# A retention and swish kernel on one core: batches 0 and 1 load their keys and values two positions a partition

## The chip, the core and the metric

The kernel runs on one core of a Trainium2 chip. TensorE (PE) multiplies matrices, VectorE (DVE), ScalarE (ACT) and GpSimd (POOL) work element by element, and SyncE (SP) issues nearly all DMAs. The metric is the device time of one execution, in microseconds. It is given as the median of several runs; the profile comes from one further execution.

## The reference

The kernel computes a retention layer over 8 batches, 8 heads, 576 positions and a head size of 64, and then a dense block with a swish in it:

```python
scores = scale * np.matmul(q, k.transpose(0, 1, 3, 2))
gamma = 1.0 - 2.0 ** (-5.0 - np.arange(H, dtype=np.float32))
rel = pos[:, None] - pos[None, :]
Dmat = np.where(rel >= 0, gamma[:, None, None] ** rel[None, :, :], 0.0)
attn_out = np.matmul(scores * Dmat[None, :, :, :], v)
x = attn_out.transpose(0, 2, 1, 3).reshape(B * S, H * D)      # 4608 x 512
h = x @ w_in                                                  # 512 x 2048
g = h * (1.0 / (1.0 + np.exp(-beta * h)))
return (g @ w_out).astype(np.float32)                         # 2048 x 512
```

All inputs and the output are float32 in DRAM. The kernel works in bf16 on TensorE.

## The kernel before

The decay factorizes: gamma to the power (i - j) is a gain on query i (`gq`) times a gain on value j (`gv`), so each batch needs only a causal mask. The first 512 positions of a batch are four chunks of 128; the last 64 of all batches together form a ninth block. A chunk's output has two parts: scores of the chunk against itself, masked and multiplied with its values (`a_sc`, `a_O`), and the queries times a state, the sum of key-value products of all chunks before it (`a_st`, `a_cross`). The output of the four chunks of a batch stands transposed in `xT`, and is the input of the dense block: 16 "ups" (`up`, `ups`) of four matmuls of 512 columns each, whose result goes through a Silu on ScalarE into `gT`, and then "downs" (`down`). From block 3 on the downs are done by a scheme with seven products in place of eight (`seven_mm`).

Queries lie four positions a partition: position 4 s + i is in partition s, slot i, so that a chunk of 128 positions is a group of 32 partitions (`PC`) in each of four slots. A DMA of q moves pieces of 1 KB (`load_q`, L77 to L87, two DMAs of 512 KB, by halves of the heads). Keys and values of batches 0 and 1 (`b < QB`) lie one position a partition, so `load_kv` (L89 to L105) moves pieces of 256 bytes; a chunk's keys and values share one tile `kvn` of 512 KB, of which there are six. Batches 2 to 7 use another layout with half chunks side by side, and are not touched.

Batches 0 and 1 work by chunk. For each chunk `pre` (L330) casts the keys to bf16 (`kn`, L364) and multiplies the values with `gv` (`vn`, L336), both on GpSimd; `t_k` (L391) transposes the keys on TensorE and copies them out of PSUM into `kT`; `a_sc` (L403) makes the scores of a chunk in 8 matmuls with 64 rows and 128 columns of the array and masks them on VectorE into `R` (L417); `a_O` (L449) makes 8 matmuls with 128 rows and 64 columns; `a_st` (L474) adds to the state in 4 matmuls of the whole array and copies its two diagonal blocks into `sbd`; `a_cross` (L437) multiplies the state with the queries; `a_x` (L464) copies the output into `xT`. `t_q` (L384) transposes the scaled queries that `pre_q` (L310) writes. `warm_up` (L259) issues float32 matmuls on zeros as fillers.

Every engine runs its instructions in the order in which the program issues them. The order for batch 0 is written out by hand (L869 to L915). The rest is a list `fill` of TensorE steps in order, with side steps merged in: each side step has a due place in that list (`streams`, L957 to L972; `merged`, L857), `d0` being the place of the first down and `u1` that of batch 1's first up. SP's queue has the same order. PSUM has eight banks, held by tag: "mm" three, "O" two, "sc" two, "st" one; a step waits until the bank that it takes over has been copied out.

The weights come behind batch 0: eleven DMAs of `w_in` (`load_w_in`, L192) in eight pieces, 4 MB in all, cast to bf16 by GpSimd and VectorE in turn (`cast_w_in`, L201), then `w_out`. The first ups need the cast of the first piece. Batch 1's loads follow `w_out` at place 10.3 of the list, and batch 2's follow them.

Of the kernel before, what the change touches and what calls it, by code (L numbers as in the profile page):

```python
# [19 lines left out]
def kernel(  # L20
# [54 lines left out]
    q_tiles, kv_tiles = {}, {}  # L75
# [13 lines left out]
    def load_kv(n, js=(0, 1)):  # L89

        if n >= len(full):
            return
        b, c = seq[full[n]]
        if 0 in js:
            kv_tiles[full[n]] = stage.tile([P, 2, H, D], F32, name="kvn", tag="kvn", bufs=NQ)
        t = kv_tiles[full[n]]
        for j in js:
            src = (k, v)[j][b].rearrange("h s d -> s h d")
            if b < QB:
                nc.sync.dma_start(t[:, j], src[c * P:(c + 1) * P])  # L100
            elif c % 2 == 0:
# [6 lines left out]
    ahead = [(0, 0), (0, 1), (1, 0), (1, 1), (2, 0), (3, 0), (2, 1), (3, 1)]  # L108
    keys_first = [(0, 0), (1, 0), (0, 1), (1, 1), (2, 0), (3, 0), (2, 1), (3, 1)]
# [12 lines left out]
    load_q(0)  # L122
    for n, j in ahead:
        load_kv(n, (j,))
# [9 lines left out]
    for j, (step, mul) in enumerate(((1, CB), (P, 1))):  # L134
        nc.gpsimd.iota(pos[:, j, :CB], pattern=[[step, CB]], base=0, channel_multiplier=mul,
# [10 lines left out]
    for h in range(H):  # L146
# [12 lines left out]
    causal = consts.tile([P, P], BF16, name="causal")  # L159
    nc.gpsimd.memset(causal[:], 1.0)  # L160
    nc.gpsimd.affine_select(out=causal[:], in_=causal[:], pattern=[[1, CB], [CB, PC]], compare_op=ALU.is_ge,
                            fill=0.0, base=0, channel_multiplier=-1)
# [38 lines left out]
    def cast_w_in(g, kos=None):  # L201
        t = wts[g]
        f0, fn, rows = pieces[g]
        for ko in kos or range(rows[0].start, rows[-1].stop):
            if ko % 2 == 0:
# [59 lines left out]
    def betas():  # L265
        pb = psum.tile([P, FO], F32, name="pb", tag="mm", bufs=3)
        nc.tensor.transpose(pb[:], beta_rows[:], ident_f[:FO, :FO])
        nc.scalar.copy(beta_sb[:], pb[:])
# [24 lines left out]
    def row_of(b, c):  # L293
        return CB + 1 + c % 2 * 2 + c // 2 if b >= QB else c
# [35 lines left out]
    def pre(i, js=(0, 1)):  # L330

        b, c = seq[i]
        if 0 not in js:
            v, g = kv_tiles.pop(i)[:, 1], gains(gv, row_of(b, c))
            if b < QB:
                nc.gpsimd.tensor_tensor(live[i]["vn"][:], v, g, ALU.mult)  # L336
            else:
                by_halves(live[i]["vn"], v, g)
# [24 lines left out]
        for to, hs in turned if b >= QB else [(slice(0, H), slice(0, H))]:  # L363
            nc.gpsimd.tensor_copy(kn[:, c % 2, to], t[:, 0, hs])  # L364
        if 1 in js:
            pre(i, (1,))

# [16 lines left out]
    def t_q(b, u):  # L384
        T = psum.tile([P, CB, 2, P], BF16, name="T", tag="mm" if u else "O", bufs=3 if u else 2)
        for i in range(CB):
            for p in range(2):
                nc.tensor.transpose(T[:, i, p, :], heads(batch[b]["qs"][:, i], 2 * u + p), ident[:])
        (nc.vector.tensor_copy if u else nc.scalar.copy)(batch[b]["qT"][:, :, 2 * u:2 * u + 2], T[:])

    def t_k(i):  # L391
        T = psum.tile([P, HP, P], BF16, name="T", tag="sc" if i in (CB + 2, CB + 3) else "O", bufs=2)
        for p in range(HP):
            nc.tensor.transpose(T[:, p, :], heads(live[i]["kn"], p), ident[:])
        (nc.vector.tensor_copy if i in (CB + 2, CB + 3) else nc.scalar.copy)(live[i]["kT"], T[:])
# [7 lines left out]
    def a_sc(i):  # L403
        L = live[i]
        L["R"] = R = sb.tile([P, 2, HP, P], BF16, name="R", tag="R", bufs=3)

        tag = "mm" if i == CB - 1 else "O" if i >= E and (i - E) % 2 else "sc"
        sc = [psum.tile([P, HP, P], F32, name="sc", tag=tag, bufs=3 if tag == "mm" else 2) for _ in range(2)]
        for p in range(HP):
            for j in range(2):  # L410
                r = slice(j * D, (j + 1) * D)
                rhs, view = q_cols(i, r, p)
                nc.tensor.matmul(view(sc[j][:, p, :]), L["kT"][r, p, :], rhs, start=True, stop=True,  # L413
                                 skip_group_check=True)
        m_b = causal[:].unsqueeze(1).to_broadcast([P, HP, P])
        for j in range(2):
            nc.vector.tensor_tensor(R[:, j], sc[j][:], m_b, ALU.mult)  # L417

    def split(i):
        return i in (CB - 1, CB + 1)  # L420

    def new_O(i):
        b, c = seq[i]
        if split(i):
            tags = ("sc", "sc") if i == CB - 1 else ("O", "sc")
            live[i]["O"] = [psum.tile([P, 2, P], F32, name="O", tag=t, bufs=2) for t in tags]
# [22 lines left out]
    def a_O(i):  # L449

        b, c = seq[i]
        L = live[i]

        early = i < E
        if not early:
            new_O(i)
        R, vn = L["R"], L["vn"]
        crossed = c > 0
        for j, p in [(n % 2, n // 2) for n in range(H)]:
            nc.tensor.matmul(O_of(i, p)[j * D:(j + 1) * D], vn[:, 2 * p + j, :], R[:, j, p, :],  # L460
                             start=opens(i, p) and not (early and crossed), stop=early or not crossed,
                             skip_group_check=True)

    def a_x(i):  # L464
# [3 lines left out]
        if split(i):  # L468
            nc.vector.tensor_copy(x[:, :2], view(Os[0]))
            nc.scalar.copy(x[:, 2:], view(Os[1]))  # L470
# [3 lines left out]
    def a_st(i):  # L474

        b, c = seq[i]
        L = live[i]
        if c == 0:
            state_ps[b] = psum.tile([P, HP, P], F32, name="st", tag="st", bufs=1)
        st = state_ps[b]  # L480
        for p in range(HP):
            nc.tensor.matmul(st[:, p, :], heads(L["kn"], p), heads(L["vn"], p),
                             start=(c == 0 and p == 0), stop=True, skip_group_check=True)
        for j in range(2):
            r, cols = slice(j * D, (j + 1) * D), slice(j * D, (j + 1) * D)
            e = nc.vector.tensor_copy if i in (CB + 2, CB + 3) else nc.scalar.copy
            if c < CB - 1:
                e(sbds[c][r, :, cols], st[r, :, cols])
                continue
            e(ends[b][r, :2], st[r, :2, cols])  # L490
            e(ends[b][(1 - j) * D:(2 - j) * D, 2:], st[r, 2:, cols])
# [331 lines left out]

    pos_, ots, held = {}, {}, []
# [44 lines left out]
    warm_up(5)  # L869
    betas()  # L870
    betas_safe()
    for n in range(4):
        pre_q(0, n)
    t_q(0, 0)
    warm_up(1, 128)
    t_q(0, 1)
    pre(0)
    t_k(0)
    warm_up(2, 128)
    a_sc(0)  # L880
    a_st(0)
    pre(1)
    t_k(1)
    warm_up(1, 128)
    a_cross(0, True)
    a_O(0)
    a_x(0)
    a_sc(1)
    a_cross(1, True)
    pre(2, (0,))  # L890
    t_k(2)
    a_st(1)
    a_O(1)
    pre(3, (0,))
    a_sc(2)
    t_k(3)
    a_x(1)
    warm_up(1, 128)
    a_sc(3)
    a_cross(2, True)  # L900
    pre(2, (1,))
    a_st(2)
    a_O(2)
    a_x(2)
    pre(3, (1,))
    warm_up(2, 128)
    a_cross(3, True)
    a_O(3)
    cast_w_in(0, (0, 1))
    a_x(3)  # L910
    cast_w_in(0, (2, 3))
    a_st(3)
# [10 lines left out]
    fill = [F(ups, 0, (fo, fo + 1), u, tags) for fo, tags in ((0, ("mm", "mm")), (2, ("O", "O")), (4, ("sc", "sc"))) for u in range(2)]  # L923
# [27 lines left out]
    def second(i):  # L951
        for f in (a_O, lambda j: a_cross(j, False), a_x):
            f(i)
            f(i + 1)
        a_st(i + 1)
# [5 lines left out]
               [(10.3, F(load_q, 1))] + [(10.3, F(load_kv, CB + n, (j,))) for n, j in keys_first],  # L961
# [145 lines left out]
```

## Time and profile before

| | us |
|---|---|
| median of 3 runs (291.51 to 293.75) | 291.57 |
| the profiled execution | 292.41 |
| its span on the core | 290.7 |

| stretch of the span | what TensorE does there |
|---|---|
| 0 to 18.44 | fillers and batch 0's retention |
| 18.44 to 32.34 | ups of batch 0 |
| 32.34 to 42.70 | downs of batch 0 |
| 42.70 to 55.95 | batch 1's retention between downs of batch 0 and ups of batch 1 |
| 55.95 to 287.3 | ups, downs and the retention of the other batches |

A line of the order of work has start, duration, engine, line of the kernel, instruction, output tile, input tiles, shape and count; neighbouring instructions of one kind are merged, and brackets give the engine's idle time before and what ended it. The end of a matmul is modelled, some 0.17 us behind the last column, so two groups overlap in the list; differences of starts tell more. A line of the waits has the waiting instruction, what it waited for, the sum in us, how many times and the longest.

### The profile page before, as it was taken

To read this page: it belongs to the slowest core of one execution; us is meant where nothing else is said; L and a number is where in the kernel's file an instruction comes from. 1 tells how busy PE (TensorE), PEld (TensorE's weight loads), DVE (VectorE), ACT (ScalarE), POOL (GpSimd) and SP (SyncE) were. 2 spreads that over 40 slices of the span, in tenths; PEclk is the share of its full clock that TensorE was granted. 3 is DMA by queue.
4 is the path that set the end of the run, shared out by engine and by line. 5 is a ranking of instruction groups with operands and counts; after the bars stand their busy time and mean duration, and the time that the engine had idled before them with its cause. 6 is when DMAs were issued, how large, how long until landed. Compare 5 with 4: busy or idle time off the path is not lost.

```text
span 290.7 us, 8297 instructions
## 1 busy us (share of the span) xinstructions
PE 281.9 (97%) x3433; PEld 175.7 (60%) x3433; DVE 186.1 (64%) x340; ACT 171.5 (59%) x301; POOL 139.1 (48%) x259
## 2 busy tenths in 40 slices
PE   8799999999999998999999999999999999999995
PEld 6554446864544554448854885578547845784584
DVE  6563555804896396279889875995597555642673
ACT  5677546686878872765158625772576156837730
POOL 4766207872499397089759539625088100000000
PEclk9999999999999999999999999999999999999999
DMA  8999999996989999988999989990779430003004
GB/s 213 218 342 386 387 283 233 240 190 123 247 180 246 253 187 201 267 225 214 183 249 265 195 231 260 189 156 2 215 176 142 92 144 3 2 28 119 0 4 143
DMA packets 128886, 54.03 MB, mean 186 GB/s; under 512 B 110400, under 2 KB 121680, under 8 KB 128848
## 3 DMA queue, kind: packets, MB, share of 16 engines
q1 hardware_dynamic: 128816, 53.49, 77.9%
q8 instruction: 27, 0.44, 0.7%
q14 instruction: 11, 0.09, 0.1%
q10 hardware_dynamic: 32, 0.01, 0.0%
HBM read 36.71 MB, written 9.44 MB: 159 GB/s over the span
## 4 chain that ended last, share of the span: by engine, by line
PE 55%; DVE 5%; POOL 4%; DMA 2%; issue 1%; ACT 0%; SPq 0%; DVEq 0%
PE ph L727 27%; PE U L764 10%; PE Z L764 7%; PE W L764 6%; DMA qn<-in_q_dram 2%; DVE sa L748 2%; PE O L509 2%; PE po L837 2%; POOL vn L305 2%; POOL kn L364 1%; PE sc L509 1%; POOL qs L323 1%; PE st L509 1%; DVE gT L732 1%; DVE R L286 1%
## 5 line engine op out<-in xcount | busy, mean ns | idle before, releaser
L727 PE MATMUL ph<-xT,w_in_sb 128*128 128x512 bf16 (+1 forms) x560 | 116.8, 364 | 0.0
L727 PEld LDWEIGHTS <-w_in_sb 128*128 128x128 bf16 x560 | 53.3, 98 | 55.2 <-POOL w_in_sb L206 0.7
L734 ACT ACTIVATE gT<-ph,beta_sb 128x512 bf16<-128x512 f32 (+1 forms) x92 | 58.4, 642 | 42.6 <-PE ph L727 41.8
L764 PEld LDWEIGHTS <-sa 128*128 128x128 bf16 x480 | 46.9, 98 | 5.8 <-issue 0.2
L732 DVE TENSOR_SCALAR gT<-hs,ratio 128x512 bf16<-128x512 f32 x48 | 25.8, 538 | 32.9 <-ACT hs L731 32.6
L364 POOL CAST kn<-kvn 128x128 bf16<-128x128 f32 (+2 forms) x80 | 35.8, 483 | 22.3 <-DMA kvn<-in_k_dram 21.8
L323 POOL TENSOR_TENSOR qs<-qn,gq 128x256 bf16<-128x256 f32 x48 | 30.5, 667 | 33.2 <-DMA qn<-in_q_dram 23.4
L748 DVE TENSOR_TENSOR sa<-gT 128x1024 bf16<-128x1024 bf16 (+1 forms) x54 | 43.9, 854 | 1.4 <-PE Z L764 1.2
L731 ACT ACTIVATE hs<-ph,beta_sb 128x512 f32<-128x512 f32 x48 | 33.0, 688 | 19.0 <-PE ph L727 18.7
L837 PE MATMUL po<-w_out_sb,gT 128*128 128x512 bf16 x192 | 43.5, 379 | 0.0
L305 POOL TENSOR_TENSOR vn<-kvn,gv 128x256 bf16<-128x256 f32 x48 | 34.3, 739 | 1.2 <-DMA kvn<-in_v_dram 0.7
L837 PEld LDWEIGHTS <-gT 128*128 128x128 bf16 x192 | 18.1, 98 | 20.6
L764 PE MATMUL U<-b,sa 128*128 128x256 bf16 x192 | 22.9, 272 | 0.1
L764 PE MATMUL Z<-b,sa 128*128 128x256 bf16 x192 | 22.9, 273 | 0.0
L286 DVE TENSOR_TENSOR R<-sc,late 128x512 bf16<-128x512 f32 x24 | 15.4, 681 | 11.4 <-issue 10.2
L764 PEld LDWEIGHTS <-gT 128*128 128x128 bf16 x192 | 18.7, 98 | 3.5
L248 DVE TENSOR_TENSOR b<-wt 128x512 bf16<-128x512 f32 x20 | 16.4, 880 | 1.9 <-ACT wt L231 1.8
L417 DVE TENSOR_TENSOR R<-sc,causal 128x512 bf16<-128x512 f32 x16 | 10.2, 686 | 4.6 <-PE sc L413 4.5
L819 PE MATMUL ph<-xT,w_in_sb 128*128 128x512 bf16 x56 | 12.4, 379 | 0.2 <-ACT xT L470 0.2
L642 ACT CAST xT<-O 128x512 bf16<-128x512 f32 x19 | 9.8, 599 | 3.5 <-PE O L509 3.5
L764 PE MATMUL W<-b,gT 128*128 128x256 bf16 x96 | 11.5, 273 | 0.0
L764 PE MATMUL U<-b,gT 128*128 128x256 bf16 x96 | 11.5, 273 | 0.0
(118 smaller groups left out, 304.8 us busy)
## 6 DMA issues: line engine op xcount, KB each, us to landing
qn<-in_q_dram SPq DMA_DIRECT2D x16, 512.0 KB, 5.8
out_dram<-ot SPq DMA_DIRECT2D x32, 256.0 KB, 3.3
kvn<-in_k_dram SPq DMA_DIRECT2D x20, 256.0 KB, 5.4
kvn<-in_v_dram SPq DMA_DIRECT2D x20, 256.0 KB, 5.1
wt<-in_moe_w_out_dram SPq DMA_DIRECT2D x8, 512.0 KB, 9.3
kvn<-in_k_dram SPq DMA_DIRECT2D x24, 128.0 KB, 4.0
kvn<-in_v_dram SPq DMA_DIRECT2D x24, 128.0 KB, 3.4
wt<-in_moe_w_in_dram SPq DMA_DIRECT2D x5, 512.0 KB, 8.2
```

Of the source, the lines that this page charges most:

```text
L248: nc.vector.tensor_tensor(to, x, y, op)
L286: return lambda: f(*a)
L305: nc.gpsimd.tensor_tensor(vn[:, hs], v[:, hs], g[:, hs], ALU.mult)
L323: nc.gpsimd.tensor_tensor(batch[b]["qs"][:, cs, to], q_tiles[b][:, hs, cs].rearrange("p h i d -> p i h d"), gq[:, cs, hs].unsqueeze(3).to_ ...
L364: nc.gpsimd.tensor_copy(kn[:, c % 2, to], t[:, 0, hs])
L727: nc.tensor.matmul(ph, w_in_sb[:, ko, fo * P:(fo + 1) * P], xts[m][:, ko, :, w], start=(ko == 0), stop=(ko == KO - 1))
L731: nc.scalar.activation(h, ph, ACT.Silu, scale=beta_sb[:, fo:fo + 1])
L732: nc.vector.tensor_scalar(gts[m][:, fo], h, ratio[:, fo // 2:fo // 2 + 1], None, ALU.mult)
L734: nc.scalar.activation(gts[m][:, fo, :, w], ph, ACT.Silu, scale=beta_sb[:, fo:fo + 1])
L748: nc.vector.tensor_tensor(sums_a[0][:, held_in[j], ks], quarter(m, *x, ks), quarter(m, *y, ks), op)
L764: nc.tensor.matmul(chains[c, n][:, 0 if alone else p], a, sevens[k // 2][:, j - 1, k % 2, :], start=j in (3, 4, 1) and k == 0 and (alone o ...
L837: nc.tensor.matmul(po[:, :nn], gT[:, fo, ms, :], w_out_sb[:, fo, n0:n0 + nn], start=(fo == 0), stop=(fo == FO - 1))
```

## The change

Batches 0 and 1 load keys and values by spans of 256 positions, two positions a partition (`load_span`): position 2 p + r of a span is in partition p, slot r. A DMA moves 512 KB in pieces of 512 bytes, and a tile holds either keys or values. Batch 0's order of loads is: first q half, first keys, second q half, last keys, first values, last values. The rows of `pos` and the mask `causal` follow the layout; the mask now has two slots of 128.

In this layout a half of the partitions of a span is a chunk. So `a_sc`, `a_O` and the states work on 64 x 64 parts of the array, and `a_sc(b, u, y)` makes the scores of both chunks of span u for half of the head pairs, y. The state after chunk 0 and that after chunk 1 are made in one step (`states(b, 0)`) in two parts of one bank. `state_out` does the copies.

Some work changes its engine. In batch 0 one cast of keys is on VectorE and one on ScalarE (before: GpSimd), one product of values is on VectorE, some of the copies of transposes change between ScalarE and VectorE, `beta_sb` is copied by VectorE, chunk 2's output is copied by VectorE alone, and the first piece of `w_in` is cast three parts by GpSimd and one by VectorE. The first filler is one call, then `betas`, then three more.

The first two ups are done by halves of the tokens (`up_spans`): chunks 0 and 1 first, 256 columns a matmul, then chunk 3's state, then chunks 2 and 3. Batch 1's steps come in five groups in place of more, smaller ones: key transposes of span 0 at d0 + 12.6; both scores of span 0 with the first two states at d0 + 14; key transposes of span 1 and the outputs of span 0 at d0 + 15.85 and 15.9; scores of span 1 with the third state at u1 + 1; outputs of span 1 and the last state at u1 + 8.

The diff, cut to its core:

```diff
+    def load_span(b, u, j):
+        t = stage.tile([P, H, 2, D], F32, name="kvn", tag="kvn", bufs=NQ)
+        nc.sync.dma_start(t[:].rearrange("p h r d -> p h (r d)"),
+                          (k, v)[j][b][:, 2 * u * P:2 * (u + 1) * P].rearrange("h (p r) d -> p h (r d)", r=2))
+        span_tiles[b, u, j] = t
...
-    load_q(0)
-    for n, j in ahead:
-        load_kv(n, (j,))
+    load_q(0, (0,))
+    load_span(0, 0, 0)
+    load_q(0, (1,))
+    load_span(0, 1, 0)
+    load_span(0, 0, 1)
+    load_span(0, 1, 1)
...
+    def pre_k(b, u, r, copy=nc.gpsimd.tensor_copy):
...
+        copy(spans[b, u]["kn"][:, r], span_tiles[b, u, 0][:, :, r])
+
+    def pre_v(b, u, r, multiply=nc.gpsimd.tensor_tensor):
+        vn = spans[b, u]["vn"][r] = sb.tile([P, H, D], BF16, name="vn", tag="vn", bufs=7)
+        multiply(vn[:], span_tiles[b, u, 1][:, :, r], gains(gv, 2 * u + r), ALU.mult)
...
+    def t_q(b, u, cs=slice(0, CB), copy=None):
...
+        (copy or (nc.vector.tensor_copy if u == b else nc.scalar.copy))(batch[b]["qT"][:, cs, 2 * u:2 * u + 2], T[:])
+
+    def t_k(b, u, r):
+        late_span = b and u
...
+        (nc.vector.tensor_copy if late_span or b == 0 and u != r else nc.scalar.copy)(spans[b, u]["kT"][:, r], T[:])
...
+    def a_sc(b, u, y, step=None):
...
+        tag = ("O" if b else "mm") if y else "sc"
+        sc = [psum.tile([P, 2, 2, P], F32, name="sc", tag=tag, bufs=3 if tag == "mm" else 2) for _ in range(2)]
+        def one(j, r, pp, x):
+            rhs, view = q_cols(b * CB + 2 * u + x, row_d(j), 2 * y + pp)
+            mm(view(sc[j][half(x), r, pp, :]), L["kT"][row_d(j), r, 2 * y + pp, half(x)], rhs, start=True)
+        paired(*[[F(one, j, r, pp, x ^ j) for r in range(2) for pp in range(2) for x in range(2)] for j in range(2)])
...
+    def a_O(b, u, y, crossed=(), last=True):
+        L = spans[b, u]
+        def one(x, pp, r, hh):
+            i, p = b * CB + 2 * u + x, 2 * y + pp
+            mm(O_of(i, p)[row_d(hh)], L["vn"][r][half(x), 2 * p + hh, :], L["R"][y][half(x), hh, r, pp, :],
+               start=opens(i, p) and r == 0 and x not in crossed, stop=last and r == 1)
+        paired(*[[F(one, x, pp, r, hh ^ x) for pp in range(2) for r in range(2) for hh in range(2)] for x in range(2)])
...
+    def states(b, c):
...
+        for n, rows in ((0, half(0)), (1, slice(0, P))) if c == 0 else ((1, half(c % 2)),):
+            for r in range(2):
+                for p in range(HP):
+                    for j in range(2):
+                        mm(st[row_d(j), n, p, :], L["kn"][rows, r, 2 * p + j, :], L["vn"][r][rows, 2 * p + j, :],
+                           start=c == 0 and n == 0 and p == 0 and r == 0, stop=r == 1)
...
+    def up_spans(fs, u):
...
+        w = slice(u * 2 * PC, (u + 1) * 2 * PC)
+        for kos in (range(2), range(2, KO)):
+            for f in fs:
+                for ko in kos:
+                    nc.tensor.matmul(phs[f][:, :, w], w_in_sb[:, ko, f * P:(f + 1) * P], xts[0][:, ko, :, w],
+                                     start=u == 0 and ko == 0, stop=ko == KO - 1, skip_group_check=True)
...
+    warm_up(1)
     betas()
     betas_safe()
+    warm_up(3)
+    for n in range(2):
         pre_q(0, n)
     t_q(0, 0)
+    pre_k(0, 0, 1, nc.vector.tensor_copy)
+    pre_k(0, 0, 0)
+    t_k(0, 0, 1)
+    t_k(0, 0, 0)
+    for n in range(2, 4):
+        pre_q(0, n)
     warm_up(2, 128)
+    a_sc(0, 0, 0, 0)
+    t_q(0, 1, slice(0, 2), nc.scalar.copy)
+    t_q(0, 1, slice(2, CB), nc.vector.tensor_copy)
+    a_sc(0, 0, 0, 1)
+    pre_k(0, 1, 0)
+    pre_k(0, 1, 1, nc.scalar.copy)
+    warm_up(2, 128)
+    t_k(0, 1, 0)
+    t_k(0, 1, 1)
+    pre_v(0, 0, 0)
+    pre_v(0, 0, 1, nc.vector.tensor_tensor)
+    a_sc(0, 0, 1)
+    warm_up(2, 128)
+    a_sc(0, 1, 0)
+    states(0, 0)
+    state_out(0, 0)
+    state_out(0, 1)
+    for r in range(2):
+        pre_v(0, 1, r)
+    for c in range(2):
+        new_O(c)
+    a_O(0, 0, 0)
+    a_O(0, 0, 1, last=False)
     a_x(0)
+    a_sc(0, 1, 1)
+    a_cross(1, False)
     a_x(1)
+    warm_up(2, 128)
     a_cross(2, True)
+    new_O(3)
+    states(0, 2)
+    state_out(0, 2)
+    cast_w_in(0, (0, 1, 2), True)
+    cast_w_in(0, (3,))
+    a_O(0, 1, 0, (0,))
+    a_O(0, 1, 1, (0,))
+    a_cross(3, False)
     a_x(2)
     a_x(3)
+    up_spans((0, 1), 0)
+    states(0, 3)
+    state_out(0, 3)
     cast_w_in(1)
...
     def second(i):
+        for f in (new_O, lambda j: a_O(1, j % CB // 2, j % 2, last=False), lambda j: a_cross(j, False), a_x):
             f(i)
             f(i + 1)
...
+               [(d0 + 8, F(pre_k, 1, 0, r)) for r in range(2)] + [(d0 + 9, F(pre_v, 1, 0, r)) for r in range(2)] +
+               [(d0 + 12.6, F(t_k, 1, 0, 0)), (d0 + 12.6, F(t_k, 1, 0, 1)), (d0 + 14, F(a_sc, 1, 0, 0)), (d0 + 14, F(a_sc, 1, 0, 1)),
+                (d0 + 14, F(states, 1, 0)), (d0 + 14, F(state_out, 1, 0)), (d0 + 15.9, F(second, 4))],
+               [(d0 + 10, F(pre_k, 1, 1, r)) for r in range(2)] + [(d0 + 12, F(pre_v, 1, 1, r)) for r in range(2)] +
+               [(d0 + 15.85, F(t_k, 1, 1, 0)), (d0 + 15.85, F(t_k, 1, 1, 1)), (u1 + 1, F(a_sc, 1, 1, 0)), (u1 + 1, F(a_sc, 1, 1, 1)),
+                (u1 + 1, F(states, 1, 2)), (u1 + 1, F(state_out, 1, 2)), (u1 + 8, F(second, 6))]]
```

More of the change, by code (lines that the diff above doesn't have):

```diff
@@ L424, in new_O @@
         if split(i):
[L425 to L426 removed]
+            live[i]["O"] = [psum.tile([P, 2, P], F32, name="O", tag=t, bufs=2) for t in (("O", "sc") if b else ("sc", "O"))]
         else:
```

177 lines of the change are left out of this document (63 added, 114 removed).

## The prediction

> **What bounds the kernel now.** I read the page's busy times first, then TensorE's waits, then the order of work in the first 20 us engine by engine, and last the two later places where TensorE stands still or where batch 1 is worked off.
>
> ```profile
> PE 281.9 (97%) x3433; PEld 175.7 (60%) x3433; DVE 186.1 (64%) x340; ACT 171.5 (59%) x301; POOL 139.1 (48%) x259
> ```
>
> TensorE is busy 97%, so what counts is when its useful work starts, how much matmul time there is, and its few stalls. Its order of work at the start (start, duration, line, tile, count, [idle before]):
>
> ```profile
> 1.25 4.64 PE L262 MATMUL ph<-warm 128*128 128x256 f32 x10 [1.25 <-DVE warm L130]
> ...
> 8.84 0.66 PE L262 MATMUL ph<-warm 128*128 128x128 f32 x4
> ...
> 17.52 0.41 PE L460 MATMUL O<-R,vn 128*64 128x128 bf16 x8
> 17.87 0.40 PE L482 MATMUL st<-vn,kn 128*128 128x128 bf16 x4
> 18.44 5.34 PE L819 MATMUL ph<-xT,w_in_sb 128*128 128x512 bf16 x24 [0.17 <-ACT xT L470]
> 23.70 1.90 PE L727 MATMUL ph<-xT,w_in_sb 128*128 128x512 bf16 x8
> 25.43 7.07 PE L819 MATMUL ph<-xT,w_in_sb 128*128 128x512 bf16 x32
> 32.34 10.53 PE L837 MATMUL po<-w_out_sb,gT 128*128 128x512 bf16 x48
> ```
>
> From 18.44 to 32.34 stand 64 ups in 13.9 us, 217 ns each: solid. Before 18.44 TensorE only looks busy, with fillers; the time is set by batch 0's chain through the other engines. VectorE in that stretch:
>
> ```profile
> 4.76 1.29 DVE L326 TENSOR_TENSOR qs<-qn,gq 128x512 bf16<-128x512 f32 x2 [0.46 <-DMA qn<-in_q_dram]
> 6.23 1.31 DVE L326 TENSOR_TENSOR qs<-qn,gq 128x512 bf16<-128x512 f32 x2 [0.17 <-DMA qn<-in_q_dram]
> 8.03 0.69 DVE L389 COPY qT<-T 128x1024 bf16<-128x1024 bf16 x1 [0.49 <-PE T L388]
> 10.18 1.29 DVE L417 TENSOR_TENSOR R<-sc,causal 128x512 bf16<-128x512 f32 x2 [1.46 <-PE sc L413]
> ```
>
> It has gaps: key and value tiles come in late. The rates by window (after the engines' columns: clock, DMA share, GB/s) show why:
>
> ```profile
> 3.00:4.00 1.00, 1.00 (x4) 0.73 (x4) 1.00 (x6) 0.51 (x3) 0.72 (x3) 1.00 1.08 368
> 9.00:10.00 1.00, 0.82 (x12) 0.53 (x11) 0.00 (x0) 0.59 (x1) 0.85 (x2) 1.00 1.35 217
> ```
>
> q, in pieces of 1 KB, moves at 368 GB/s; k and v, in pieces of 256 bytes, at 217: 1.2 us for each 256 KB. The longest stall past 60 us, in the waits and in TensorE's order:
>
> ```profile
> PE st L509 <- POOL vn L305: 1.3, 2, 1.0
> ```
>
> ```profile
> 110.03 0.19 PE L509 MATMUL st<-vn,kn 64*64 64x64 bf16 x1 [1.03 <-POOL vn L305]
> ```
>
> GpSimd's order leads back from there: values for batch 4 at 108.94, behind its q at 99.31, whose load SP issues at 94.68 behind a transpose that waits for GpSimd's work on batch 3, and so on to batch 2's q, issued at 47.32 behind batch 1's loads. TensorE's pace is not in that chain as I read it; the loads of batch 1 are.
>
> **Loads.** A span has 1024 pieces of 512 bytes in place of two tiles with 1024 of 256. No row has 512. Per DMA engine a piece takes 18.8 ns at 256 bytes (217/16 GB/s) and 44.5 ns at 1 KB (368/16); the straight line between gives 27.4 ns, 299 GB/s, 1.75 us a span against 2.4. Bounds: 217 (no gain) and 368 (1.42 us). I take 1.75, between the two rows. Each batch then saves 4 x 0.65 = 2.6 us of loading. Landings: first q half 4.7 (VectorE starts on it at 4.76), first keys 6.4, second q half 7.9 (1.45 each, from 4.76 to 6.23), last keys 9.6, values 11.4 and 13.1, against some 15.8 for the last values now (14.70 for the third tile, plus 1.2). w_in follows 2.6 us earlier.
>
> [...] The two rows agree that 256 is slow; none decides about 512.
>
> **Batch 0 up to the first ups.** Loads land earlier, but copies move to VectorE. Its list behind the first transposes of q: q copy 0.69 (from ScalarE, L389 row), keys 0.43 (the 128x512 cast to bf16 at L208), a wait of 0.49 for the transposes (0.39 and two handovers of 0.05, as between the rows at L364, L394 and L395), key copy 0.42, q half 2 x 0.65, eight masks 8 x 0.65, half a q copy 0.42, key copy 0.42, values 0.65 (as L326), one w_in cast 0.33, 0.2 for the last outputs, three output copies 3 x 0.42. Together 11.8 us. It starts once the first q transposes are done: TensorE has pb at about 3.3, when beta and the identity are there, then six filler passes of 464 ns (the x10 row) to 6.4, then 0.6: 7.05. So 18.85 for the last copy of VectorE. Of 12.4 us between 6 and 18.4 VectorE now works 8.0; the move adds 3.2 and fills it.
>
> ScalarE's list ends beside it: first states at 14.2 (values on VectorE done at 13.3, 0.85 of matmuls), then three state copies of 0.76 and two outputs of 0.59, 17.85 for the last, and the crossing that it releases 18.1. The ups by halves start there: 8 of 256 columns (109 ns each) and a state, 1.1 us, hide the copies until 18.85; second half from 19.25, both ups done 20.1. Now they are done at 18.44 + 8 x 0.217 = 20.2. Gain 0.1. Bounds: if the fillers end at 6.0, all is 0.5 earlier and ScalarE's tail shorter (-0.8); if GpSimd and VectorE slow each other as they do at 77.86 (0.8 us for a 0.58 us instruction), or TensorE's steps show between VectorE's, +0.5. Earlier loads are worth nothing beyond that here, and cost +1.3 where a span takes 2.4 us. The w_in casts come earlier than their ups; the mask's second affine select (0.3) and the other iota patterns lie under GpSimd's idle 2.6 us before 6.39; without it the first keys would be late by 0.3.
>
> **Batch 1 among the downs and ups.** Here every TensorE us counts.
>
> ```profile
> 46.19 1.04 PE L837 MATMUL po<-w_out_sb,gT 128*128 128x512 bf16 x4
> 47.16 0.40 PE L413 MATMUL sc<-qT,kT 64*128 64x128 bf16 x8
> ...
> 48.69 0.67 PE L460 MATMUL O<-R,vn 128*64 128x128 bf16 x16
> 49.28 0.40 PE L446 MATMUL O<-qT,sbd 128*128 128x128 bf16 x4
> 49.52 0.39 PE L482 MATMUL st<-vn,kn 128*128 128x128 bf16 x4
> 49.74 0.39 PE L394 MATMUL T<-ident,kn 128*128 128x128 bf16 x4
> 50.09 0.61 PE L727 MATMUL ph<-xT,w_in_sb 128*128 128x256 bf16 x4
> ```
>
> Starts show 0.1 us lost at each change of tile shape (four downs are 0.87, the next start is 0.97 later). From 42.70 to 55.95 stand four groups of downs (3.5) and seven of ups (3.05), so attention has 6.7 us. Afterwards: transposes 1.75 as now, scores 64 matmuls of 128 columns at about 14 ns (8.4 at 64 columns: 32 in 0.27 us at 67.76), outputs the same, states 64 x 14 in three places, crossings 0.65, and about ten changes of shape in place of some sixteen: 6.0. Saved 0.7. But the state and the transposes at 49.52 and 49.74 now cover the copies of batch 1's first outputs; afterwards they lie ahead of the outputs, and up 0 follows the crossing at once. The copies end (0.17 drain, 0.59 and 0.39 on ScalarE) some 1.0 us after the outputs, the crossing takes 0.3: stall 0.7. Scores right behind the key copies of ScalarE (2 x 0.59 against 1.3 of cover) may cost 0.2 more. Sum +0.2, from -0.5 (copies overlap) to +0.7 (no matmul time saved).
>
> **The late stall.** Batch 2's q lands 2.6 + 2.6 = 5.2 us sooner, and the chain on GpSimd and SP with it, unless it meets SP's order. It needs 1.35 at 110. I take all: -1.35 (bounds 0 and -1.55, all idle between 100 and 200 us).
>
> Sum -0.1 + 0.2 - 1.35 = -1.25. The profiled execution took 292.41 (span 290.7 and 1.7 around), 0.84 above the median of the runs; on it that is 291.15, on the median 290.3.
>
> **Rivals.** (1) Slower: TensorE stays at its slow start. The x10 row has 464 ns for 256 columns, the later filler 165 ns for 128 with the drain, 123 without, so full speed is 245: the first eight or so ran at half speed, to about 5.3. After the change two passes are followed by a second of waiting for beta and six more. If full speed has not come by 8, the 8 us of matmuls up to 18.1 become 16, in 11.7 us: +4, 294.3 with the late stall gone and 295.7 with it. The x10 row speaks for it; the six passes and the transposes right behind them, 4 us together, against. [...] Chance 0.14. (2) The late stall stays, since SP's stores (3.18 us at 90.05) or buffers hold the chain: 291.6. Chance 0.18. (3) Batch 0 follows its loads, 2.6 us earlier, and the stall goes: 287.8. Speaks for it: the ups' w_in comes as much earlier; against: VectorE's list. Chance 0.17. (4) The spans load no faster, the change doing nothing to the rate: +1.3 and +0.2, 293.1. Chance 0.05. My forecast: 0.46, from -0.8 - 0.5 - 1.55 = 288.7 to 292.0.
>
> **The numbers.** 290.3 us; 288.0 to 293.3 leaves out most of (1) and half of (3). About 1%, 2.9 us, is what counts as a change: faster than 288.7 has (3) and a tail of the forecast, 0.22; slower than 294.5 has two thirds of (1) and small tails, 0.13; the rest 0.65, mostly a little faster.
>
> **What would show it.** In the profile after: spans landing 1.75 us apart; VectorE without gaps from 7 to 19 and first ups done at 20.1; a stall of 0.7 before batch 1's first up; no wait for L305 at 110. If the first ups are done before 19, or the first transposes show 100 ns each, or the wait at 110 is there, that step was wrong.

## The result and the profile after

In the comparison that goes with the prediction the changed kernel takes 294.96 us (median of 20 runs, 292.54 to 297.1), the kernel before 293.01 (20 runs, 291.09 to 296.98). The ratio is 1.0065, 95% interval 1.0036 to 1.0094: slower by about 1.9 us. Two later comparisons of the same two kernels gave 0.997 (0.9928 to 1.0011) and 1.0071 (1.0036 to 1.0106). Some runs of both kernels had a mean granted clock below 0.996 (7 of the 20 of the changed kernel in the first comparison, 10 of the 23 of the kernel before beside the second, 2 of 19 beside the third) and took 1.6 to 3.3 us more at the median; without them the medians of the second are 293.4 and 293.2. So the changed kernel lies within about 1% of the kernel before, rather above it than below. Forecast was 1.3 us less. The forecast of 290.3 us started from 291.57, the median of three runs; the 20 runs of the comparison have 293.01, so 1.4 of the 4.7 us between 290.3 and 294.96 are in the base, and 3.2 in the effect of the change.

The profiled execution took 292.54 us, span 290.8. It was the shortest of its 20, and it hides most of the loss. Each kernel was therefore profiled twice more, and this table has the times of four places of TensorE's order in all six executions (us from the start of the span; in brackets the time of that execution):

| | before (292.41) | second (293.26) | third (295.62) | changed (292.54) | second (293.48) | third (293.98) |
|---|---|---|---|---|---|---|
| first down of batch 0 | 32.34 | 32.57 | 32.60 | 34.07 | 33.92 | 33.99 |
| first scores of batch 2 | 67.76 | 67.99 | 68.02 | 69.88 | 69.73 | 69.80 |
| last scores | 237.18 | 237.94 | 240.39 | 237.32 | 238.25 | 238.73 |
| span | 290.7 | 291.5 | 293.9 | 290.8 | 291.8 | 292.2 |

Up to batch 2 the changed kernel is behind by 1.7 to 2.1 us, in every execution. From there to the last scores it needs 167.4, 168.5 and 168.9 us, against 169.4, 170.0 and 172.4: it gains, by an amount that changes from execution to execution. Behind the last scores both need 53.5. The time is the sum of a fixed loss and a gain that comes and goes.

The busy times of the changed kernel, first profile:

```profile
PE 278.3 (96%) x3637; PEld 176.7 (61%) x3665; DVE 183.0 (63%) x347; ACT 169.2 (58%) x298; POOL 131.0 (45%) x258
```

28 records of matmuls are missing from this trace (3637 against 3665 weight loads); by its weight loads TensorE has 232 matmuls more than before. It is busy 3.6 us less, of which 2.4 lie in the first 22 us (16.26 against 18.64). Its order of work from 16.8 us to the end of the first two ups shows where:

```profile
16.88 0.27 PE L476 MATMUL O<-qT,sbd 128*128 128x128 bf16 x2 [0.32 <-ACT xT L498]
17.08 0.38 PE L539 MATMUL st<-vn,kn 64*64 64x64 bf16 x12
...
17.34 0.40 PE L539 MATMUL O<-R,vn 64*64 64x128 bf16 x12
19.13 0.47 PE L539 MATMUL O<-R,vn 64*64 64x128 bf16 x18 [1.39 <-issue]
19.52 0.40 PE L476 MATMUL O<-qT,sbd 128*128 128x128 bf16 x4
19.76 1.04 PE L864 MATMUL ph<-xT,w_in_sb 128*128 128x256 bf16 x8
20.73 0.44 PE L539 MATMUL st<-vn,kn 64*64 64x64 bf16 x16
21.10 1.05 PE L864 MATMUL ph<-xT,w_in_sb 128*128 128x256 bf16 x8
21.98 3.62 PE L849 MATMUL ph<-xT,w_in_sb 128*128 128x512 bf16 x15
```

In the middle of a run of 32 equal outputs, behind the 14th, TensorE stands still for 1.39 us, and "issue" says that it waited for nothing that the profile shows. The masks it reads ended at 16.77, the state copies at 18.30, the copies of the outputs before at 17.31: no data became ready near 19.13. The first two ups are done at 21.98, before at 20.2.

The rates by window, and GpSimd's order (start, duration, line, instruction):

```profile
9.00:10.00 1.00, 0.82 (x21) 0.54 (x20) 1.00 (x3) 0.58 (x1) 0.00 (x0) 1.00 1.20 291
10.00:11.00 1.00, 0.92 (x16) 0.75 (x12) 1.00 (x3) 0.58 (x2) 0.61 (x1) 1.00 1.19 289
```

```profile
10.34 0.61 POOL L379 CAST kn<-kvn 128x512 bf16<-128x512 f32 x1 [3.05 <-DMA kvn<-in_k_dram]
12.22 1.55 POOL L384 TENSOR_TENSOR vn<-kvn,gv 128x512 bf16<-128x512 f32 x1 [1.28 <-DMA kvn<-in_v_dram]
```

Pieces of 512 bytes move at 289 to 298 GB/s from 8 to 12 us (217 with 256 bytes). Values land at 12.2 where 11.4 was forecast, and their product takes 1.55 us, with VectorE's own product of values beside it from 12.19 on; the first such product of the kernel before took 1.04. All of TensorE's waits behind 24 us:

```profile
PE po L882 <- issue: 0.8, 5, 0.2
PE ph L757 <- issue: 0.6, 4, 0.2
PE ph L757 <- DVE xT L495: 0.4, 1, 0.4
```

The late stall behind GpSimd's values is gone. The first two lines are no waits, as far as the trace tells: these two groups have 26 of the missing records, and each piece of 0.2 us is about the 0.217 of one matmul. The third line is the wait before batch 1's first up.

### The profile page after: what moved, and what is told of

Read it like the earlier page. It is cut to its first block, busy times and chain, and to the rows that moved or that the text cites. A ratio compares the mean times of both kernels' runs of the same rounds, so it can differ in the third digit from the quotient of the medians.

```text
span 290.8 us, 8728 instructions
## 1 busy us (share of the span) xinstructions
PE 278.3 (96%) x3637; PEld 176.7 (61%) x3665; DVE 183.0 (63%) x347; ACT 169.2 (58%) x298; POOL 131.0 (45%) x258
## 4 chain that ended last, share of the span: by engine, by line
PE 90%; DMA 3%; DVE 2%; issue 2%; SPq 1%; ACT 1%; POOL 1%; DVEq 0%; POOLq 0%
PE ph L757 37%; PE po L882 14%; PE U L794 11%; PE W L794 7%; PE Z L794 7%; PE O L539 4%; PE ph L849 4%; DMA kvn<-in_v_dram 3%; PE st L539 2%; PE sc L539 2%; PE ph L864 1%; DVE sum L575 1%; SPq L109 1%; POOL vn L384 1%; PE O L476 0%
## 5 line engine op out<-in xcount | busy, mean ns | idle before, releaser
L757 PE MATMUL ph<-xT,w_in_sb 128*128 128x512 bf16 (+1 forms) x542 | 113.8, 363 | 1.9 <-issue 0.6
L757 PEld LDWEIGHTS <-w_in_sb 128*128 128x128 bf16 x560 | 53.5, 98 | 55.6 <-DVE xT L495 0.6
L882 PE MATMUL po<-w_out_sb,gT 128*128 128x512 bf16 x184 | 42.0, 379 | 1.0 <-issue 0.8
L778 DVE TENSOR_TENSOR sa<-gT 128x1024 bf16<-128x1024 bf16 (+1 forms) x54 | 40.6, 794 | 1.7 <-PE Z L794 1.5
L312 POOL TENSOR_TENSOR vn<-kvn,gv 128x256 bf16<-128x256 f32 x48 | 31.6, 681 | 6.4 <-PE O L539 3.3
L367 POOL CAST kn<-kvn 128x128 bf16<-128x128 f32 (+1 forms) x72 | 26.6, 406 | 16.3 <-DMA kvn<-in_k_dram 16.3
L882 PEld LDWEIGHTS <-gT 128*128 128x128 bf16 x192 | 18.1, 98 | 20.8
L255 DVE TENSOR_TENSOR b<-wt 128x512 bf16<-128x512 f32 x20 | 15.2, 818 | 1.9 <-ACT wt L238 1.8
L889 ACT COPY ot<-po 128x512 f32<-128x512 f32 x9 | 5.3, 584 | 10.9 <-PE po L882 10.9
L794 PE MATMUL W<-b,sa 128*128 128x256 bf16 x96 | 11.5, 273 | 0.0
```

The source lines that it names most:

```text
L312: nc.gpsimd.tensor_tensor(vn[:, hs], v[:, hs], g[:, hs], ALU.mult)
L757: nc.tensor.matmul(ph, w_in_sb[:, ko, fo * P:(fo + 1) * P], xts[m][:, ko, :, w], start=(ko == 0), stop=(ko == KO - 1))
L778: nc.vector.tensor_tensor(sums_a[0][:, held_in[j], ks], quarter(m, *x, ks), quarter(m, *y, ks), op)
L794: nc.tensor.matmul(chains[c, n][:, 0 if alone else p], a, sevens[k // 2][:, j - 1, k % 2, :], start=j in (3, 4, 1) and k == 0 and (alone o ...
L882: nc.tensor.matmul(po[:, :nn], gT[:, fo, ms, :], w_out_sb[:, fo, n0:n0 + nn], start=(fo == 0), stop=(fo == FO - 1))
```

## The experiments

**The gap: instructions or data?** My guess for the wait without a releaser was the supply of instructions. No view shows that supply itself; the nearest row is the instruction queue of the page, which moved 27 packets of 16 KB before and 28 after. I call such a packet the refill. The DMA view of the changed kernel finds one of them between 16.4 and 16.5 us, 2.7 us ahead of the end of the gap:

```profile
q8 instruction: 1, 0.02, 68.0%
```

Ahead of the gap stand 223 matmuls with 223 weight loads. Both kernels ran once more unchanged, and the changed one with bf16 fillers in four places (eight matmuls of 128 columns each):

> The changed kernel once more, unchanged. Theory A (instruction supply): TensorE has used up its instructions when it reaches the 15th of the 32 output matmuls of span 1, because the 64 x 64 matmuls use up two program rows in 14 ns each; the gap with no releaser comes again at the same matmul, 1 to 3 us long, and the first ups are done near 22. Theory B (a data wait that the trace doesn't show): the gap comes again at the same matmul too, but with the same 1.4 us. Theory C (an accident of one execution): no gap there, first ups done at 20.6. Time by A and B: 292.5 to 297, median near 295, as in the runs of the changed kernel so far; the execution profiled then, 292.5, was the shortest of 20.

> The kernel before once more, for a second profile. All theories: 291 to 297 us, no gap without a releaser over 0.3 us in the first 33 us, the late stall at 110 (1.0 to 1.4 us at the state matmul behind GpSimd's values) there again, first ups done at 20.2.

```diff
-    warm_up(2, 128)
+    filler(8)
```

> The four short fillers of batch 0 (two float32 matmuls each, two program rows, 0.5 us) become eight bf16 matmuls of 128 columns each (sixteen rows, 0.5 us): the same TensorE time, 56 program rows more ahead of the place of the gap. Theory A: the gap comes 56 rows, 28 matmuls, earlier, so among the state matmuls or crossings between 16.2 and 17.2, and no longer at the 15th output. Theory B: it stays at the 15th output. Theory C: no gap. Time within 1 us of the changed kernel by all three.

The changed kernel again, 293.46 us (12 runs), and with other fillers, 294.95 (10 runs, ratio to before 1.0008, 0.9963 to 1.0053). TensorE's order, first of the unchanged one, then of the one with other fillers:

```profile
18.19 0.40 PE L539 MATMUL O<-R,vn 64*64 64x128 bf16 x12
18.98 0.47 PE L539 MATMUL O<-R,vn 64*64 64x128 bf16 x18 [0.40 <-issue]
```

```profile
17.55 0.41 PE L544 MATMUL st<-vn,kn 64*64 64x64 bf16 x14
19.98 0.26 PE L544 MATMUL st<-vn,kn 64*64 64x64 bf16 x2 [2.02 <-issue]
19.98 1.10 PE L544 MATMUL O<-R,vn 64*64 64x128 bf16 x32
```

The gap came again behind the 14th output, 0.40 us long where 1 to 3 had been expected, with the work ahead of it 0.9 us later. With other fillers it left that place and stood behind 14 of the 16 state matmuls, 16 matmuls earlier and not the 28 expected: I had counted a float32 filler as two program rows, and the trace shows two matmuls and two weight loads for each, so 32 rows were added and not 56. Counted so, the gap opened behind the 223rd matmul in both. A data wait would have stayed with its matmul: that theory falls. The packet moved at 16.5 to 16.75 and at 17.25 to 17.5, and the gap ended 2.4 and 2.6 us behind it. The kernel before gets its first packet at the same time (16.2 to 16.8 us in its three profiles), but it comes to its 223rd matmul only behind 33 us and has no such gap.

**What the refill waits for.** Two kernels were to move the packet, one by less data ahead of it, the other by asking earlier. The first loads one piece of w_in ahead, and the rest behind a small DMA that reads the second state's copy:

```diff
-    for g in range(NP):
-        load_w_in(g)
+    load_w_in(0)
...
     state_out(0, 1)
+    nc.sync.dma_start(hold[:], sbds[1][:, 0, :16])
+    for g in range(1, NP):
+        load_w_in(g)
```

> The changed kernel with only the first piece of w_in loaded ahead; the other ten DMAs are issued behind the copy of the second state (about 16 us), by a small DMA that reads it. DMA is then idle from about 15.4 to 17. If the refill waits behind data in the DMA queues, the instruction packet that moved at 16.4 comes at 15.4 or before, the gap ends 1 us earlier and is 0.4 us or none. If the refill takes its time whatever the data, packet and gap stay. The ups behind may wait for w_in, so the whole time says nothing.

The second adds 32 matmuls of 32 columns with 32 columns of weights:

```diff
     t_q(0, 0)
+    tiny_rows(32)
```

> The changed kernel with 32 very small matmuls (64 program rows, some 25 ns each) in TensorE's pause at 7.2. If the refill is asked for when TensorE has used a certain number of rows, some 6 to 7 us ahead of the packet, it is asked for 2 us earlier: the packet moves at about 14.5 instead of 16.4 and there is no gap although the place of it comes 32 matmuls earlier. If the packet's time hangs on the data traffic alone: packet at 16.4 to 16.6, and the gap comes 32 matmuls earlier, from about 16.7, and is 2 us long or more.

The order of work around the old place of the gap, first with w_in held back, then with the early rows:

```profile
17.79 0.62 PE L539 MATMUL O<-R,vn 64*64 64x128 bf16 x30
18.80 0.40 PE L476 MATMUL O<-qT,sbd 128*128 128x128 bf16 x4 [0.39 <-ACT sbd L518]
```

```profile
17.10 0.62 PE L544 MATMUL O<-R,vn 64*64 64x128 bf16 x30
18.11 0.40 PE L481 MATMUL O<-qT,sbd 128*128 128x128 bf16 x4 [0.39 <-ACT sbd L523]
18.35 1.04 PE L869 MATMUL ph<-xT,w_in_sb 128*128 128x256 bf16 x8
19.31 0.44 PE L544 MATMUL st<-vn,kn 64*64 64x64 bf16 x16
19.68 1.05 PE L869 MATMUL ph<-xT,w_in_sb 128*128 128x256 bf16 x8
20.57 3.62 PE L854 MATMUL ph<-xT,w_in_sb 128*128 128x512 bf16 x16
```

The packet moved at 14.0 to 14.25 and at 13.75 to 14.0, and in both the 32 outputs run through: no gap, as expected. So, by one execution of each, the refill's time moves with both, the traffic on the DMA queues and how early TensorE uses up its rows: it came some 2.3 us earlier with w_in held back (229 GB/s in the window of the packet, where the changed kernel has 348 from 14 to 15 us) and some 2.5 earlier with 64 more rows (398 GB/s in the window of the packet). The 6 to 7 us from the asking to the packet were my estimate; no view shows when it is asked for. In place of the gap the last crossing waits 0.39 us for ScalarE's state copies. Holding w_in made ups wait for it later (295.97 us, one run). With the early rows the first ups are done at 20.57 and the one run took 292.01 us, beside a median before of 293.01. Adding 64 useless instructions took 1.4 us off batch 0 in that execution.

**What else batch 0 costs.** Two reorderings:

```diff
-    warm_up(1)
+    warm_up(2)
     betas()
...
     t_q(0, 0)
+    warm_up(1)
+    warm_up(1, 128)
```

> The changed kernel with fillers in TensorE's two early pauses: one more float32 filler ahead of beta (1 us at 2.5) and one and a half behind the first transposes of q (0.75 us at 7.2). Theory of the clock: the transposes and scores from 8.4 to 13 are at 80 and 14 ns in every execution, where one profile of the changed kernel showed 100 to 120 ns there; the first outputs start at 14.6. The end of the gap stays at 19 to 19.2 all the same, as the instructions set it, so the gap is longer, 1.5 us, and the time is that of the changed kernel within 0.5 us. Rival: the slow stretch sets the time of the first ups, which are then done 1 us earlier, near 20.9. Place of the gap: 6 matmuls earlier, as 12 rows are added.

```diff
+    up_spans((0, 1), 0)
     a_O(0, 1, 0, (0,))
     a_O(0, 1, 1, (0,))
     a_cross(3, False)
     a_x(2)
     a_x(3)
-    up_spans((0, 1), 0)
```

> The changed kernel with the first half of the first two ups (8 matmuls of 256 columns, 0.9 us) moved ahead of the 32 outputs of span 1, where TensorE ran out of instructions. Instruction supply: sixteen rows then take 0.9 us instead of 0.2, the place of the gap comes 0.7 to 0.9 us later and the gap is that much shorter (about 0.5 where it was 1.4, none where it was 0.4), and the first ups are done 0.7 us earlier, near 21.2; the gap, if any, stands still at TensorE's 223rd matmul. Rival: the gap keeps its length behind whatever stands ahead of the outputs. Ratio to before about 0.998.

The fillers: 293.46 us, ratio 0.9969 (0.9937 to 1.0001). The expectation was wrong about the gap: it went, with the packet at 15.0 to 15.25; the 12 added rows are early ones, which fits the run with early rows. The slow stretch (below, 107 ns a transpose in place of 56) was not there; the first ups were done at 21.37 in that execution, since the values landed late and the first states waited 0.81 for GpSimd, until 14.38. The ups ahead of the outputs: 293.99 us, ratio 1.005 (1.0007 to 1.0093). The gap shrank to 0.84 and opened behind the 222nd matmul listed; its end stayed at 19.12, and the first ups were done at 21.52, 0.46 earlier instead of 0.7. Their ratio is no better than the changed kernel's.

The slow stretch that the expectation for the fillers puts down to the clock, key transposes of the changed kernel, first and second profile:

```profile
8.35 0.62 PE L414 MATMUL T<-ident,kn 128*128 128x128 bf16 x8 [1.12 <-DVE kn L379]
```

```profile
8.51 1.03 PE L414 MATMUL T<-ident,kn 128*128 128x128 bf16 x8 [1.12 <-DVE kn L379]
```

Eight transposes in 0.62 and in 1.03 us, 56 and 107 ns each without the drain of 0.17. The slow stretch (to 11 or 13 us) is in three of the ten profiles with the changed batch 0, in none of the four with batch 0 as before, though the granted clock reads 1.00 all along. With no gap, the first ups were done at 21.26 in the execution that had it (w_in held) and at 20.57 in the one that had not (early rows); the two differ in their loads and rows as well.

**Batch 1 alone.** Batch 0 as before, batch 1 as changed (its loads below, and all its steps), with rows of `pos` and a mask of its own for the spans:

```diff
-               [(10.3, F(load_q, 1))] + [(10.3, F(load_kv, CB + n, (j,))) for n, j in keys_first],
+               [(10.3, F(load_q, 1))] + [(10.3, F(load_span, 1, u, j)) for u in range(2) for j in range(2)],
```

> Batch 0 as in the kernel before (its loads, order and copies), batch 1 by spans as in the changed kernel. If the changed kernel lost its gain in batch 0 (instruction supply): no gap without a releaser before the first ups, first ups done at 20.2, batch 1 0.4 us longer than before, the late stall gone (its chain starts from batch 1's loads, 2.6 us shorter), together about 1.0 us less than before, ratio 0.9965. Rival: the late gain came from batch 0's earlier loads, and with batch 1's alone the late stall stays: ratio 1.001.

It took 294.72 us (12 runs), ratio 1.0006 (0.997 to 1.0042): the expectation failed, and its rival, that the stall stays, came close. The waits of TensorE behind 24 us:

```profile
PE T L428 <- POOL kn L387: 1.0, 2, 0.8
PE st L604 <- POOL vn L316: 0.9, 2, 0.8
PE st L604 <- POOL vn L392: 0.6, 1, 0.6
PE ph L822 <- DVE sum L640: 0.4, 1, 0.4
PE ph L822 <- DVE xT L541: 0.4, 1, 0.4
```

No gap, first ups as before (downs from 32.41). But batch 1's keys and values came too late for the five groups (1.0 and 0.6 us), and the late stall was still 0.9. SP issued batch 2's q at 44.60, between 47.32 before and 41.79 in the changed kernel. The mask of its own adds three instructions on GpSimd, which may have a part in the first waits. Batch 1's tight order needs the time that batch 0's faster loads give it: alone, this half of the change does not pay. Batch 0's half alone was not run.

**The late stall, and what follows a long one.**

> The kernel before for a third profile. The first showed the stall of 1.35 us behind GpSimd's values at 110, the second none there, but 1.8 us of stalls behind VectorE's sums and output tiles after 122. If the stall at 110 is the rule, it is here (54.8 us from batch 2's first scores to batch 4's, as in the first; 53.2 in the second); if it is one form of a loss that shifts from execution to execution, the sum from batch 2's first scores to the last scores (169.4 and 170.0 us) is within 1 us of these either way.

The waits of TensorE behind 24 us in the third profile of the kernel before, and its clock there (after the engines' columns: clock, DMA share, GB/s):

```profile
PE st L509 <- POOL vn L305: 2.5, 2, 2.2
PE st L509 <- issue: 0.5, 1, 0.5
```

```profile
112.00:113.00 1.00, 1.00 (x57) 0.66 (x44) 0.43 (x1) 0.36 (x1) 1.00 (x5) 0.57 0.35 15
113.00:114.00 1.00, 1.00 (x4) 0.34 (x3) 1.00 (x3) 0.72 (x2) 1.00 (x4) 0.50 1.20 264
114.00:115.00 1.00, 1.00 (x3) 0.30 (x2) 0.97 (x3) 0.00 (x0) 1.00 (x2) 0.50 1.16 247
115.00:116.00 1.00, 1.00 (x5) 0.47 (x4) 0.93 (x5) 0.08 (x1) 0.81 (x2) 0.72 1.11 269
```

The stall was 1.35 us in the first profile, absent in the second, 2.5 in the third, and there the granted clock was 0.57, 0.50, 0.50 and 0.72 in the four us from 112 on, behind it. Neither form of the expectation holds: it is neither the rule nor worth the same each time (169.4, 170.0, 172.4 us). In the second, other stalls stood in its place behind 122 us: VectorE's sums (1.1) and an output tile (0.7).

**A third profile, and two combinations.**

> The changed kernel unchanged, for a third profile and a third comparison; the first gave a ratio to before of 1.0065, the second 0.997. Theory: two losses set an execution's time, the gap in batch 0 (with half clock behind it when the gap is 2 us or more) in the changed kernel, and the stall behind GpSimd's values at 110 (with half clock behind it when it is 2 us or more) in the kernel before; the median ratio lies between 0.997 and 1.0065 according to how often each happens on the chip. The profile shows the gap at the 223rd matmul again and no stall behind GpSimd's values at 110. Rival: the first comparison is what the change costs, and ratio and profile show 1.9 us more than before, from a loss that neither of the two profiles so far has.

294.76 us (8 runs), ratio 1.0071 (1.0036 to 1.0106), above the band: the ratio is the rival's, the profile is not. It (293.98) has the gap at the same matmul, 1.74 us, no stall behind GpSimd's values, and small ones that neither profile had before: 0.76 without a releaser at 104.5, 0.43 behind an output tile at 171.

The combinations have the extra fillers or the small matmuls, the first ups ahead of span 1's outputs, and batch 1's second key transposes moved:

```diff
-               [(d0 + 15.85, F(t_k, 1, 1, 0)), (d0 + 15.85, F(t_k, 1, 1, 1)), (u1 + 1, F(a_sc, 1, 1, 0)), (u1 + 1, F(a_sc, 1, 1, 1)),
+               [(d0 + 15.95, F(t_k, 1, 1, 0)), (d0 + 15.95, F(t_k, 1, 1, 1)), (u1 + 1, F(a_sc, 1, 1, 0)), (u1 + 1, F(a_sc, 1, 1, 1)),
```

> The changed kernel with three edits: the fillers of the run with steady fillers (no gap there), the first half of the first two ups ahead of span 1's outputs, and batch 1's second key transposes moved from ahead of the first outputs to behind them (places d0 + 15.85 to d0 + 15.95), which is again cover for the copies of those outputs. Theory (the gap and, right behind it, the wait of the last crossing for ScalarE's state copies cost batch 0 its time; the lost cover costs batch 1 0.4 us): no gap, first ups done at 20.7 to 20.9, no stall before batch 1's first up, 1.5 us less than the changed kernel, ratio to before 0.994 to 0.998. Rival: ScalarE's and VectorE's lists alone set the first ups at 21.3 or later; then 0.4 to 0.8 us less than the changed kernel, ratio about 0.998 to 1.001.

> The best kernel so far with the 32 very small matmuls in place of the extra fillers: the changed kernel, these matmuls at 7.2, the first half of the first ups ahead of span 1's outputs, and batch 1's second key transposes behind its first outputs. Theory: no gap (packet at 14), first ups done at 20.5 or earlier, no stall before batch 1's first up, ratio to before 0.995 to 1.0. Rival: without the extra filler ahead of beta the transposes at 8.4 run at half speed in some executions; then up to 1 us more in these.

With the extra fillers: 292.74 us (12 runs, 291.56 to 293.64), ratio to before 0.9991 (0.9964 to 1.0017). With the small matmuls: 293.15, ratio 1.002 (0.9997 to 1.0043). TensorE's order in the first, around the first ups and where batch 1's first up stands:

```profile
18.06 0.64 PE L539 MATMUL O<-R,vn 64*64 64x128 bf16 x32
18.63 0.40 PE L476 MATMUL O<-qT,sbd 128*128 128x128 bf16 x4
18.96 0.44 PE L539 MATMUL st<-vn,kn 64*64 64x64 bf16 x16
19.66 1.03 PE L864 MATMUL ph<-xT,w_in_sb 128*128 128x256 bf16 x8 [0.26 <-DVE xT L495]
20.53 3.62 PE L849 MATMUL ph<-xT,w_in_sb 128*128 128x512 bf16 x16
...
49.77 0.40 PE L476 MATMUL O<-qT,sbd 128*128 128x128 bf16 x4
50.00 0.61 PE L414 MATMUL T<-ident,kn 128*128 128x128 bf16 x8
50.58 0.61 PE L757 MATMUL ph<-xT,w_in_sb 128*128 128x256 bf16 x4
```

No gap, first ups done at 20.53, no stall before batch 1's first up: each step as expected, and batch 2's first scores at 68.14, against 69.8 in the changed kernel. The ratio (0.994 to 0.998) was not reached: by the medians this is 0.7 to 2.2 us less than the changed kernel, beside which it was never run, but no measurable gain on the kernel before. With the small matmuls the first ups were done at 21.06 (20.5 expected), and a gap without a releaser of 0.82 us stood in batch 1's states.

## Why the prediction failed

**Loads: right.** 299 GB/s forecast, 289 to 298 measured; the first values still landed 0.8 us later than forecast. q's pieces of 1 KB moved at 351 to 358 GB/s in this trace and pieces of 256 bytes at 217 in the one before, so pieces of 512 lie between the two, as the forecast had taken it.

**Batch 0 up to the first ups: the step that failed.** "Now they are done at 20.2 ... both ups done 20.1", with bounds of -0.8 and +0.5, became 21.8 to 22.0 in the three profiles. The sum walked VectorE's and ScalarE's lists instruction by instruction and gave TensorE's own list only matmul time. It never counted the instructions: 223 matmuls by 17.7 us, where the kernel before had 143. So VectorE, which was to be without gaps from 7 to 19 us, stood still for 2.25 us ahead of its output copies. Its lines, first of the changed kernel, then the last such copy with early rows:

```profile
19.40 0.42 DVE L495 CAST xT<-O 128x256 bf16<-128x256 f32 x1 [2.25 <-PE O L539]
```

```profile
18.43 0.42 DVE L500 CAST xT<-O 128x256 bf16<-128x256 f32 x1
```

The early rows show the size: with the gap taken away and the slow stretch absent VectorE's last copy ends at 18.85, as in the sum, and the first ups are done at 20.57, 0.47 off the forecast and just within its bounds. That rest is ScalarE's last state copy, which ends at 18.05 and not 17.85, so that the ups begin at 18.35 and not 18.1, and then 2.22 us for both halves with the state where 2.0 were booked. The bounds held known costs only; a step that adds more than half to an engine's instructions should have had a term for them. The upper end of the forecast, 292.0, is also less than its own bounds add up to: 0.5, 0.7 and 0 on 291.57 are 292.8.

**Batch 1: right in mechanism.** Forecast +0.2; from the first down to batch 2's first scores 35.42 us before and 35.81 after, +0.39, the same in all three profiles of each. The stall for lost cover was 0.41, forecast 0.7. Giving the cover back removed it.

**The late stall: right that it goes, wrong that it is a fixed sum.** It is in none of the changed kernel's three profiles. But the -1.35 came from one execution; in the others it would have been 0 and -2.5 with the clock behind it. SP issued batch 2's q 5.5 us sooner (5.2 forecast), and 2.7 sooner with batch 1's loads alone, where 0.9 of the stall was left. That fits the chain that the prediction reads, but the kernel before can be without the stall too, so it is not shown. From batch 2's first scores to the last, the difference in the means of three is 2.3 us, without the third profile of before 1.4.

**The rivals.** TensorE was slow early in some executions, as the first rival has it, at a price of about 0.7 us and not 4 (an estimate from 21.26 and 20.57), and hidden under the gap where both came. That the clock made it is not shown, as its record reads 1.00 there. The stall at 110 did not stay. Batch 0 did not follow its loads. The rival on the slower side was the wrong mechanism: what stood there was the gap behind the 223rd matmul, 0.40 to 1.74 us long.

**Sum, on the first pair of profiles:** +1.73 to the first down, +0.39 for batch 1, -1.98 from there to the last scores, -0.04 behind: +0.10 in the span, where -1.25 was forecast.

One thing stays open. By the medians the change costs 1.9, -0.9 and 1.9 us in three comparisons. A stretch at a granted clock of 0.50 was profiled behind the stall at 110 in its long form and behind the gap with other fillers, never in the changed kernel itself; how often each kernel has one is not known. Why the changed kernel's median is 294.8 to 295.0 in two comparisons was not settled; its third profile shows only more small stalls.

## What to carry to other kernels

Count an engine's instructions when a change cuts its work into smaller pieces: here TensorE stood still for 0.40 to 1.74 us in a stretch that used 14 ns for a matmul and its weight load, 32 cheap matmuls more, early, took 1.4 us off batch 0 in one execution, and slow matmuls moved ahead of that stretch took off 0.46 in another. Before a stall is booked as a gain, look for it in a second and a third execution. A reordering that is tight in one place may live on the slack that another part of the same change makes.

## What was not expected of the hardware

TensorE stood still without a releaser behind the 223rd matmul (446 rows shown) in three profiles of the changed kernel (1.39, 0.40 and 1.74 us) and in the one with other fillers (2.02), and went on 2.4 to 2.7 us after a 16 KB packet of the instruction queue had moved, while data moved at 350 to 382 GB/s (first profile of the changed kernel, windows of 1 us from 16 to 20), 355 (its third, 16 to 19) and 361 (other fillers, 17 to 20). That it had run out of instructions is my reading of these runs. With early rows it passed its 223rd matmul 2.1 us behind the packet and did not stop, so this time is not the same everywhere. What asks for the packet, and what fills these 2.5 us, the trace does not show. Gaps without a releaser of 0.3 to 0.8 us also stood in later stretches of 64 x 64 matmuls, first in the third profile of the kernel before, then in the combination with small matmuls:

```profile
153.41 0.26 PE L509 MATMUL st<-vn,kn 64*64 64x64 bf16 x9 [0.49 <-issue]
```

```profile
53.34 0.28 PE L544 MATMUL st<-vn,kn 64*64 64x64 bf16 x7 [0.82 <-issue]
```

Seven of these are in the traces, and each ended 2.5 to 2.9 us behind such a packet (150.5 and 50.6 for the two shown, 101.6 for the one at 104.5 in the third profile of the changed kernel), with the packets some 10 us apart on average. So they bear the same sign, and the kernel before has this loss too; no run moved them.

A pause of TensorE of 2.02 us (other fillers, 18.0 to 20.0) and one of 2.16 (third profile of before) were each followed by some 3 us at a granted clock of 0.50; pauses of 1.03, 1.39 and 1.74 were not (1.00 in each us behind the first two, 1.0 in the mean of the third execution). With other fillers the clock is 0.93 in the mean from 17 to 20, which puts its fall, as an estimate from 1.00 and 0.50, at 19.6, 1.6 us into the pause.
